# First chunk's MLP sums over 4, 5 and 5 tiles, later casts of its weights, phases of seven units from unit 18

## The chip, the cores and the metric

The kernel runs on one core of a Trainium2 chip. The metric is the device time of one execution in microseconds (us), and lower is better. TensorE (PE in the profile, with PEld for its weight loads) multiplies, ScalarE (ACT) computes exponentials and some copies, VectorE (DVE) does the elementwise work, GpSimd (POOL) and SyncE (SP) issue transfers; SPq in a row is SP's queue of transfers.

## The reference

Two branches read the same `x` of 2048 rows by 512. Branch A is attention with 32 heads of width 16 that share one key and one value head; branch B is an MLP with 1792 hidden features (14 tiles of 128) and a squared ReLU. A sigmoid gate per row mixes them.

```python
q = (x @ wq).reshape(B, S, H, Dh); k = x @ wk; v = x @ wv
p = softmax(einsum("bhqd,bkd->bhqk", q, k) * Dh ** -0.5)
a = einsum("bhqk,bkd->bhqd", p, v).reshape(B, S, H * Dh) @ wo
h = relu(einsum("bsd,df->bsf", x, w1) + b1); b = einsum("bsf,fd->bsd", h * h, w2) + b2
g = sigmoid((x * gate_w).sum(-1)); out = g * a + (1 - g) * b
```

## The kernel before

The rows are worked in four chunks of 512 (`NC`, `CH`). The attention is cut into 1024 **units** `u`: a group of four heads, 128 keys and 256 of the 512 queries. A unit has score products on TensorE (L836), one exponential of 128 by 1024 on ScalarE (L873), and eight context products that add into one bank (L893). Half of the score products land in a single spare bank `x`, from which VectorE copies them to SBUF before ScalarE takes the exponential there (`score_copy`, L857).

All other products are **filler** (L1209), cut into **slots** of half a product each: the query projection of the four chunks (16 fillers of 12 slots, the first one before the loop), the MLP's hidden tiles (`hidden`, 12 slots: 4 row tiles by three terms, since an fp32 factor is split into a rounded part and a rest), the MLP's sums (`summed`, three slots for each hidden tile summed over, four column blocks of 128 rows), and the output projection. A **span** pairs the upper half of one filler with the lower half of the filler before, so it has as many slots as the longer of the two: 12, 15 and less at the end.

A **phase** scores `n` units while it runs slots of a span in an order from the table `PLANS`, and then runs the context products of `m` earlier units (`context`); scores run four units ahead of the contexts (`AHEAD`). `block` picks `m`. In the profile a phase ends with a run of L893 products, eight to a unit: x32, x48, x56, x64 or x72 in a row of the chain are 4, 6, 7, 8 and 9 units. Below unit 32 `block` calls `exact`, which picks sizes so that a phase ends at unit 32; after a span that carried the small norm products (L425, `late`), it takes six units; a 15-slot span takes eight, or nine once the MLP's weights are all in place (`wide`).

The order on every engine is the order in which the Python code emits instructions. A planner keeps estimated times `at_pe`, `at_act`, `at_dve` of three engines, and uses them only to decide where side work goes: `spend` puts VectorE's side jobs where its estimate fits.

**The MLP's weights** come as fp32 tiles of 256 KB, two halves (w1 and w2) of each of 14 tiles. `w_load` (L487) issues a load on SP into one of two staging places, `wf` and `stage`; `w_round` casts it into `w1p` or `w2p`, on ScalarE (L525) or VectorE (L510); `w_rest` takes the rounded part off (VectorE, L519), writes the pair to DRAM for the later chunks (L521), and marks the half as wanted, so that the next load is issued at the end of that phase. `w_ready` (L535) decides at the end of a phase whether a loaded tile may be cast: the planner's TensorE time must be more than `LANDS` = 6.0 past its value at the issue of the load. If a product needs a tile that has no cast yet, `have_round` and `have` emit the cast and the rest on VectorE at that place.

`mlp` (from L792) runs the 14 hidden tiles of a chunk in the groups of `GROUPS`; behind the first hidden tile of a group it runs the four sums of the group before. `gate` (L546) computes the sigmoid, two small exponentials on ScalarE and four small VectorE instructions for each of `g` and `omg` taken together; it stands in the list `soon`, from which `spend` and the start of a span (`begin`) take.

SP also carries the query tiles: each query filler's result is written to DRAM in two parts of 256 KB, `qs<-qr` by SP (L369) and `qs<-ql` by GpSimd; `q_load` (L446) reads a head group back in eight transfers.

Of the kernel before, what the change touches and what calls it, by code (L numbers as in the profile page):

```python
# [34 lines left out]
LW = 4 * CH // 64  # L35
LANDS, DIVIDES, WRITES, SPREADS, SURE = 6.0, 10.0, 14.0, 24.0, 1.4
PAIR, CONTEXT, TURN, EXP, COPY, LATE = 0.235, 0.429, 0.36, 0.925, 0.66, 0.3
GROUPS = (0, 1, 2, 3, 4), (5, 6, 7, 8, 9), (10, 11, 12, 13)
AHEAD = 4
WHOLE, FIRST, SECOND, LATER = range(4)  # L40
EXACT = {15: ((8, 15), (7, 15)), 12: ((7, 12), (6, 12), (4, 6)), 9: ((6, 9), (4, 5))}
# [128 lines left out]
def mix_kernel(ctx: ExitStack, tc: tile.TileContext, xT, wkv, wq, wo, w12, b1, b2, cst, out):  # L170
# [67 lines left out]
    with fast, tc.tile_pool(name="at", bufs=1) as at, \  # L238
# [211 lines left out]
        wf, since, rounded, ws = ({}, {}), ({}, {}), ({}, {}), ({}, {})  # L450
# [9 lines left out]
        at_pe, at_act, at_dve = 0.0, 0.0, 0.0  # L460
# [74 lines left out]
        def w_ready(half):  # L535
            n = len(rounded[half])
            return (n == len(ws[half]) and n in since[half] and n < min(room[half], NF)
                    and at_pe - since[half][n] > LANDS)

        def wq_round(t):  # L540
            nc.scalar.activation(wqr[:, t], wqf[t], AF.Copy)
# [166 lines left out]
        def hidden(c, f, hs):  # L708

            n = c * NF + f  # L710
            while c not in x:
                chores.pop(0)[1]()
            (wr, wl), (r, l) = have_round(0, n), x[c]

            def rest(p):
                have(0, n)
                return wl[:, p]

            begun[0] += 1

            def done(p):
                hr, hl = hs[f] = ring[n % 6]
                nc.vector.tensor_scalar(h[0], p, b1t[:, f:f + 1], 0.0, op0=OP.add, op1=OP.max)  # L723
                nc.vector.tensor_tensor(h[0], h[0], h[0], OP.mult)  # L724
                split(hr, hl, h[0])
                dve(1.9)
                room[0] += 1
                if f == NF - 1 and c < 2:
                    x_again(c + 2)

            ks = [(k, slice(k * 128, (k + 1) * 128)) for k in range(KT)]
            return ([(wr[:, p], x) for k, p in ks for x in (r[:, k], l[:, k])]
                    + [(lambda p=p: rest(p), r[:, k]) for k, p in ks], done, None)
# [47 lines left out]
        def mlp():  # L781

            before, rest = None, []
            for c in range(NC):
                for fs in GROUPS:
                    hs = {}
                    for f in fs:
                        yield hidden(c, f, hs)
                        if f == 3:
                            res[c] = keep.tile(sh, F32, name=f"res{c}", tag="r0")  # L790
                            biases.extend((c, j) for j in range(4))
                        o_ready(c)  # L792
                        if c == NC - 1:
                            ask(c, 2)
                        if f == fs[0] and before:
                            if fs == GROUPS[1] and c > 1:
                                yield from projection(c - 2)
                            yield from summed(*before)
                        elif c > 0 and f > fs[0] and osp.get(c - 1) and c - 1 not in over:
                            p = projection(c - 1)  # L800
                            if c == NC - 1:
                                rest.append(p)
                                for _ in range(3):
                                    yield next(p)
                            else:
                                yield from p
                    before = c, fs, hs
            yield from rest[0] if rest else projection(NC - 2)
            yield from summed(*before)
# [222 lines left out]
        def o_ready(c):  # L1032

            if c == 0 and not wos:
                wos.extend(xp.tile(sh, F32R, name=n, tag=t) for n, t in (("wor", "xr2"), ("wol", "xl2")))

                def load(a):
                    nc.sync.dma_start(stage(), wo[a * 256:a * 256 + 256].rearrange("(t p) n -> p t n", p=128))
                    return WRITES

                for t in range(KT):
                    if t % 2 == 0:
                        chores.append((0.0, lambda t=t: load(t // 2)))
                    later(lambda t=t: wos[0][:, t], lambda t=t: wos[1][:, t], lambda t=t: stage()[:, t % 2])
            if c > 0:
                ask(c - 1)

        def ask(c, n=KT):
            if c in asked or any((c, t) not in complete for t in range(n)) or c > len(asked):
                return  # L1050
            if c and not used[c - 1]:
                return
            asked.add(c)
            tiles = []

            def load(a):
                if a == 0:
                    tiles.extend((keep.tile(sh, F32R, name="orr", tag="r3"), xp.tile(sh, F32R, name="orl", tag="xl3")))
                m = min(2, n - 2 * a)
                i = c * NG + 4 * a  # L1060
                nc.sync.dma_start(stage()[:, :m], oTs[i:i + 2 * m].rearrange("(t u) d n -> (u d) t n", u=2))
                return DIVIDES

            for t in range(n):
                if t % 2 == 0:
                    chores.append((0.0, lambda t=t: load(t // 2)))
                later(lambda t=t: tiles[0][:, t], lambda t=t: tiles[1][:, t], lambda t=t: stage()[:, t % 2],
                      (lambda: osp.update({c: tuple(tiles)})) if t == n - 1 else None)
# [23 lines left out]
        def projection(c):  # L1092
            if c in over:
                return
            over.add(c)
            yield from wait(c)
            units = list(outproj(c, ots, *osp[c], *wos))
            yield from units[:3]
            terms, done, ahead = units[3]

            def last(p):
                done(p)
                used[c] = True

            yield terms, last, ahead
# [130 lines left out]
        def phase(slots, n, m):  # L1236
# [48 lines left out]
            for half in halves():  # L1285
                if spans > 5 and w_ready(half):
                    if at_act + 0.64 < at_pe + 0.7 + CONTEXT * m:
                        w_round(half, scalar_copy)
                    elif at_dve + 0.6 < at_pe + 0.7 + CONTEXT * m:
                        w_round(half, nc.vector.tensor_copy)  # L1290

        def exact(rest, slots, later):

            def price(rest, size, later):

                if rest == 0:
                    return 0.0, None
                options = []
                for m, n in EXACT[size]:
                    parts = [n] if n == size or rest == 4 else [n, size - n]  # L1300
                    if m * len(parts) <= rest and not (later and m == 7):
                        t = sum(TURN + CONTEXT * m + PAIR * m for k in parts)
                        options.append((t + price(rest - m * len(parts), 12, False)[0], (m, n)))
                return min(options, default=(1e9, (min(rest, 6), size)))

            return price(rest, slots, later)[1]

        def block(u):
            rest, left = total - u, span.left()
            if span.slots < 7 or left < 7:  # L1310
                m = 4 if left > 3 or left == 3 and u < total - NK else 2
                if rest - m == 2:
                    m = rest
                return min(m, rest), left
            if span.slots == 15:
                long[0] -= 1
            if rest <= 16 or u < 32:
                return exact(min(rest, 32 - u) if u < 32 else rest, left, late or u < 18)
            if left <= 9:
                return 6, left  # L1320
            if span.slots == 15:
                return 9 if wide and u > wide[0] else 8, left
            halved[0] += (total - 8 - u - 9 * long[0] + max(long[0] - 30, 0)) / max(units_left[0] - long[0] + 1, 1) - 7
            halved[0] = min(max(halved[0], -1.5), 1.5)
            if late:
                return 6, left
            if halved[0] <= -1.0:
                halved[0] += 1.0
                return 6, left
            if halved[0] >= 1.0 and len(ws[1]) >= NF:  # L1330
                halved[0] -= 1.0
                return 8, left
            return 7, left

        long = [10 * NC]
        late, halved, units_left = [], [0.0], [NC * (NF + 12) + 15 + 16]
# [10 lines left out]
        u, begun_q = 0, set()  # L1347
# [67 lines left out]
```

## Time and profile before

| | us |
|---|---|
| median of three runs | 1207.36 |
| lowest, highest | 1207.36, 1207.86 |
| the profiled execution | 1208.71 |
| its span, first to last instruction | 1206.9 |
| ACT, DVE busy | 1024.7, 672.0 |
| POOL busy | 56.9 |

The profile is that of one execution, so its times add up to its own 1208.71, of which 1.8 lie outside the span. Times in its rows count from the first instruction. A row of a timeline is start, duration, engine, line, operation and operands, and in brackets the idle time of the engine just before it with what ended it. A row of the chain of waits is start, duration and what the last-ending work waited for at that moment. The granted clock (PEclk) is the share of TensorE's full clock.

### The profile page before, as it was taken

The numbers are of one execution on the slowest core, as the hardware profiler recorded it, in microseconds if no ns is written. First come the engines' busy times: TensorE is split into PE (matmuls) and PEld (weight loads), VectorE is DVE, ScalarE is ACT, GpSimd is POOL, SyncE is SP. The second block draws the span as 40 slices with busy tenths as digits, with TensorE's granted clock in tenths as the row PEclk, the third lists the DMA queues.
The fourth block names the chain that finished last, engine by engine and source line by source line (L and its number), as shares of the span: only waits on it lengthen the run. The fifth ranks groups of instructions, "written<-read, shape, count | busy, mean of one in ns | idle before, by whom it ended". The sixth has DMA issues, their size and how long they took to land.

```text
span 1206.9 us, 31970 instructions
## 1 busy us (share of the span) xinstructions
PE 1183.6 (98%) x13814; PEld 782.7 (65%) x13815; DVE 672.0 (56%) x1110; ACT 1024.7 (85%) x1134; POOL 56.9 (5%) x101
## 2 busy tenths in 40 slices
PE   9997999999999999999999999999999999999996
PEld 4665666666666666666666666666666666666663
DVE  6774678476464744463556734553647448345543
ACT  6786899898888888888888898888888888988873
POOL 1000100000000000100000000000000000010000
PEclk9998999999999999999999999999999999999999
DMA  7656344134263422330344414221515135031101
GB/s 239 204 156 196 99 146 154 52 123 156 66 219 103 155 72 85 102 98 29 121 154 151 128 40 151 90 63 37 160 56 164 46 97 168 21 107 58 58 38 38
DMA packets 55226, 132.71 MB, mean 110 GB/s; under 512 B 14554, under 2 KB 15050, under 8 KB 54568
## 3 DMA queue, kind: packets, MB, share of 16 engines
q1 hardware_dynamic: 44232, 107.58, 28.4%
q0 software_dynamic: 10704, 22.77, 5.9%
q8 instruction: 110, 1.80, 0.7%
q14 instruction: 36, 0.29, 0.1%
q10 hardware_dynamic: 144, 0.26, 0.1%
HBM read 85.88 MB, written 40.09 MB: 104 GB/s over the span
## 4 chain that ended last, share of the span: by engine, by line
PE 94%; DMA 3%; DVE 1%; ACT 1%; issue 1%; SPq 0%; DVEq 0%; ACTq 0%
PE acc L893 37%; PE mm L1209 32%; PE s L836 18%; PE x L836 5%; DMA wf<-in_w 1%; ACT e L873 1%; DMA qs<-qr 1%; DMA xf<-in_xT 0%; PE mm L310 0%; PE mm L210 0%; DVE e L857 0%; DMA w1kept<-w1p 0%; PE s L320 0%; PE s L1028 0%; PE x L976 0%
## 5 line engine op out<-in xcount | busy, mean ns | idle before, releaser
L873 ACT ACTIVATE e<-s 128x1024 f32<-128x1024 f32 x764 | 742.9, 1023 | 99.8 <-PE s L836 97.7
L857 DVE COPY e<-x 128x512 f32<-128x512 f32 x520 | 359.3, 691 | 471.3 <-PE x L836 342.6
L893 PE MATMUL acc<-e,v_ext 128*32 128x256 f32 x8192 | 470.8, 381 | 0.0
L836 PE MATMUL s<-qa,k_aug 49*128 49x512 f32 x1528 | 427.8, 413 | 7.1 <-ACT e L873 6.9
L893 PEld LDWEIGHTS acc<-e,v_ext 128*32 128x32 f32 x8192 | 252.0, 110 | 191.3 <-issue 39.3
L873 ACT ACTIVATE e<-e 128x1024 f32<-128x1024 f32 x260 | 274.1, 1058 | 27.2 <-DVE e L857 27.0
L836 PEld LDWEIGHTS s<-qa,k_aug 49*128 49x128 f32 x1528 | 220.8, 185 | 107.8 <-ACT e L873 73.4
L1209 PE MATMUL mm<-w2p,hr 64*128 64x512 f32 x1128 | 241.7, 393 | 1.8 <-DVE w2p L510 1.2
L836 PE MATMUL x<-qa,k_aug 49*128 49x512 f32 x520 | 215.7, 415 | 3.7 <-DVE o L985 1.8
L1209 PEld LDWEIGHTS mm<-w2p,hr 64*128 64x128 f32 x1128 | 156.5, 186 | 20.0 <-DVE w2p L510 1.5
L1209 PE MATMUL mm<-xragain,w1p 64*128 64x512 f32 x448 | 120.8, 393 | 0.0
L836 PEld LDWEIGHTS x<-qa,k_aug 49*128 49x128 f32 x520 | 95.6, 184 | 37.5 <-DVE e L857 13.9
L1209 PE MATMUL mm<-xr,w1p 64*128 64x512 f32 x448 | 116.0, 393 | 0.2 <-DVE w1p L519 0.2
L1209 PEld LDWEIGHTS mm<-xragain,w1p 64*128 64x128 f32 x448 | 69.6, 186 | 5.7
L1209 PEld LDWEIGHTS mm<-xr,w1p 64*128 64x128 f32 x448 | 68.6, 186 | 5.9 <-DVE w1p L519 0.7
L1209 PE MATMUL mm<-xlagain,w1p 64*128 64x512 f32 x224 | 67.8, 392 | 0.0
L1209 PE MATMUL mm<-xl,w1p 64*128 64x512 f32 x224 | 65.7, 392 | 0.0
L1209 PE MATMUL mm<-more 64*128 64x512 f32 x216 | 58.8, 392 | 0.0
L723 DVE TENSOR_SCALAR big<-mm,b1t 128x512 f32<-128x512 f32 x56 | 41.5, 742 | 0.8 <-PE mm L1209 0.8
L724 DVE TENSOR_TENSOR big<-big 128x512 f32<-128x512 f32 x56 | 38.7, 692 | 1.9
L1209 PE MATMUL mm<-wor,orr 64*128 64x512 f32 x120 | 39.1, 400 | 0.5 <-DVE ol L1018 0.5
L1209 PE MATMUL mm<-wor,orl 64*128 64x512 f32 x120 | 38.7, 393 | 0.0
(163 smaller groups left out, 795.0 us busy)
## 6 DMA issues: line engine op xcount, KB each, us to landing
w1p<-w1kept SPq DMA_DIRECT2D x42, 512.0 KB
w2p<-w2kept SPq DMA_DIRECT2D x35, 512.0 KB
qa<-qs SPq DMA_DIRECT2D x186, 64.0 KB
w1kept<-w1p SPq DMA_DIRECT2D x14, 512.0 KB
w2kept<-w2p SPq DMA_DIRECT2D x12, 512.0 KB
qs<-qr SPq DMA_DIRECT2D x16, 256.0 KB
ress<-res POOLq DMA_DIRECT2D x4, 1024.0 KB, 4.8
qs<-ql POOLq DMA_DIRECT2D x15, 256.0 KB, 8.0
```

Of the source, the lines that this page charges most:

```text
L723: nc.vector.tensor_scalar(h[0], p, b1t[:, f:f + 1], 0.0, op0=OP.add, op1=OP.max)
L724: nc.vector.tensor_tensor(h[0], h[0], h[0], OP.mult)
L836: nc.tensor.matmul(dst.rearrange("p (a n) -> p a n", a=2), k_aug[rows, kt * 128:(kt + 1) * 128], qa[it][rows, :, q * HC:q * HC + HC], star ...
L857: nc.vector.tensor_copy(e_half(u)[:, 2 * r:2 * r + 2], x.rearrange("p (a n) -> p a n", a=2))
L873: nc.scalar.activation(e_half(u), src, AF.Exp, scale=SCALE)
L893: nc.tensor.matmul(accs[q][h * 32:(h + 1) * 32], v_ext[:, kt], es[u][:, h % 2 * 2 + h // 2], start=kt == 0 and it > 0, stop=kt == NK - 1, ...
L1209: nc.tensor.matmul((self.before if r else self).bank, a[p], b[p], start=not r and i == 0, stop=r == 1 and i == len(self.terms[1]) - 1, ski ...
```

## The change

Three edits. `GROUPS` becomes a list with an entry per chunk, and the first chunk's groups are of 4, 5 and 5 hidden tiles, not 5, 5 and 4. `w_ready` asks for twice `LANDS`. `block` no longer calls `exact` below unit 32: below unit 18 the rule is six units, and from there on the rule of all later units.

```diff
-GROUPS = (0, 1, 2, 3, 4), (5, 6, 7, 8, 9), (10, 11, 12, 13)
+GROUPS = [[(0, 1, 2, 3), (4, 5, 6, 7, 8), (9, 10, 11, 12, 13)]] + [[(0, 1, 2, 3, 4), (5, 6, 7, 8, 9), (10, 11, 12, 13)]] * 3
...
-                    and at_pe - since[half][n] > LANDS)
+                    and at_pe - since[half][n] > 2 * LANDS)
...
-                for fs in GROUPS:
+                for fs in GROUPS[c]:
...
-                            if fs == GROUPS[1] and c > 1:
+                            if fs[0] == 5 and c > 1:
...
-            if rest <= 16 or u < 32:
-                return exact(min(rest, 32 - u) if u < 32 else rest, left, late or u < 18)
+            if rest <= 16:
+                return exact(rest, left, late)
+            if u < 18:
+                return 6, left
```

**ScalarE, spans 7 to 9 (before) and 7 to 10 (change), the casts of the third and fourth w2 tile.** Before, from the cast of the second w1 tile on:

```order
L525 ACTIVATE w1p<-stage 128x512
L873 ACTIVATE e<-s 128x1024 x3
L873 ACTIVATE e<-e 128x1024
L873 ACTIVATE e<-s 128x1024
L873 ACTIVATE e<-e 128x1024
L873 ACTIVATE e<-s 128x1024
L525 ACTIVATE w2p<-wf 128x512
L873 ACTIVATE e<-s 128x1024 x5
L873 ACTIVATE e<-e 128x1024
L525 ACTIVATE w2p<-stage 128x512
```

The change, from the same cast on:

```order
L525 ACTIVATE w1p<-stage 128x512
L946 ACTIVATE accs<-acc 128x256
L873 ACTIVATE e<-s 128x1024 x3
L873 ACTIVATE e<-e 128x1024
L873 ACTIVATE e<-s 128x1024
L873 ACTIVATE e<-e 128x1024
L873 ACTIVATE e<-s 128x1024 x6
L873 ACTIVATE e<-e 128x1024
L525 ACTIVATE w2p<-wf 128x512
```

Seven exponentials stand between the two casts before, and 13 in the change; the cast of the fourth w2 tile follows seven exponentials after that, against six before.

**VectorE, the first sums over the second group of the first chunk (span 31 before, 30 in the change).** Before, behind the evaluation of a hidden tile (L203):

```order
L203 TENSOR_TENSOR hr<-big,hr 128x512
L510 CAST w2p<-wf 128x512
L857 COPY e<-x 128x512
L519 TENSOR_TENSOR w1p<-stage,w1p 128x512
L857 COPY e<-x 128x512
L519 TENSOR_TENSOR w2p<-wf,w2p 128x512
L921 TENSOR_SCALAR n<-lq 128x32
L857 COPY e<-x 128x512
L510 CAST w2p<-stage 128x512
L922 SCALAR_TENSOR_TENSOR lq,ok<-n,lq 128x32
L857 COPY e<-x 128x512
L519 TENSOR_TENSOR w2p<-stage,w2p 128x512
```

The change, at its first sums over the second group:

```order
L203 TENSOR_TENSOR hr<-big,hr 128x512
L510 CAST w2p<-wf 128x512
L857 COPY e<-x 128x512
L519 TENSOR_TENSOR w1p<-wf,w1p 128x512
L857 COPY e<-x 128x512
L519 TENSOR_TENSOR w2p<-wf,w2p 128x512
L857 COPY e<-x 128x512 x2
L723 TENSOR_SCALAR big<-mm,b1t 128x512
```

The cast of a second w2 tile and its rest, which stood before among the copies of the same phase, are gone from it: there the tile is cast on ScalarE at the end of the phase.

**VectorE, the gate (span 5 before, span 15 in the change).** Before:

```order
L857 COPY e<-x 128x512 x2
L549 TENSOR_SCALAR g<-g 128x16
L550 RECIPROCAL g<-g 128x16
L549 TENSOR_SCALAR omg<-omg 128x16
L550 RECIPROCAL omg<-omg 128x16
L857 COPY e<-x 128x512 x2
```

The change:

```order
L410 TENSOR_TENSOR sq_147<-qr 128x512
L549 TENSOR_SCALAR g<-g 128x16
L550 RECIPROCAL g<-g 128x16
L549 TENSOR_SCALAR omg<-omg 128x16
L550 RECIPROCAL omg<-omg 128x16
L857 COPY e<-x 128x512 x4
```

The four instructions move from the start of the second phase of span 5, ahead of its two copies, to the start of span 15, ahead of its four copies.

## The prediction

> **What bounds the kernel now.** I read the page first, for the engine that sets the end.
>
> ```profile
> PE 1183.6 (98%) x13814; PEld 782.7 (65%) x13815; DVE 672.0 (56%) x1110; ACT 1024.7 (85%) x1134; POOL 56.9 (5%) x101
> PE 94%; DMA 3%; DVE 1%; ACT 1%; issue 1%; SPq 0%; DVEq 0%; ACTq 0%
> ```
>
> TensorE is busy for 98% of the span and makes 94% of the chain of waits. The change takes no product away, so it can save only two things: the time in which TensorE stands still or runs slowly, and time lost between products where phases are cut badly. The waits of TensorE say where it stands.
>
> ```profile
> PE s L836 <- ACT e L873: 6.9, 2, 6.5
> PE mm L1209 <- DVE w2p L510: 1.2, 1, 1.2
> PE mm L1209 <- DVE w2p L519: 0.7, 1, 0.7
> ```
>
> One wait of 6.5 us stands out, for an exponential. The next question is what held ScalarE there, so I took its timeline, and SP's.
>
> ```profile
> 88.13 0.63 ACT L525 ACTIVATE w2p<-wf 128x512 fp32r<-128x512 f32 x1 [2.17 <-DMA wf<-in_w]
> 102.00 0.63 ACT L525 ACTIVATE w2p<-stage 128x512 fp32r<-128x512 f32 x1 [7.60 <-DMA w1kept<-w1p]
> 90.11 2.42 SPq L487 DMA_DIRECT2D stage<-in_w  x2
> 77.35 10.10 DMA wf<-in_w
> 89.36 8.81 DMA qs<-qr
> ```
>
> ScalarE stands at two weight casts, 2.17 and 7.60 us. The row of the second names the write `w1kept`, issued last before it, but the cast reads `stage`, whose loads SP issued from 90.11 on. The wait for those fits: by the chain (the last two rows), the first pair took 10.10 us from its issue at 77.35, and 90.11 to 102.00 are 11.9. A planner's distance of 6 is too short for loads that queue among the query writes, which need 8.81 us themselves. Behind the cast on ScalarE stand the exponentials of the next phase, and behind those TensorE's score banks.
>
> TensorE's own timeline shows the price, by the starts of phases. The rows of 126.51 and later are from the chain.
>
> ```profile
> 86.19 0.40 PE L425 MATMUL x<-sq,blk 128*32 128x512 bf16 x4
> 94.99 0.50 PE L836 MATMUL s<-qa,k_aug 49*128 49x512 f32 x1
> 103.86 0.80 PE L836 MATMUL s<-qa,k_aug 49*128 49x512 f32 x2 [6.50 <-ACT e L873]
> 110.97 0.43 PE s L836
> 118.73 0.43 PE s L836
> 126.51 0.22 PE x L425 x4
> 133.84 0.66 PE s L836 x2
> ```
>
> From 86.19 to 94.99 a six-unit phase behind norm products takes 8.80; the same kind takes 7.33 from 126.51 to 133.84: **1.47 lost**. From 94.99 to 110.97 a seven-unit phase takes 15.98; the next, to 118.73, takes 7.76: **8.22 lost**, 1.72 more than the idle 6.50. The stretches tell why.
>
> ```profile
> 100.00:101.00 1.00, 0.00 (x0) 0.00 (x0) 0.00 (x0) 0.00 (x0) 0.00 (x0) 0.52 0.95 381
> 105.00:106.00 1.00, 1.00 (x8) 0.81 (x6) 0.00 (x0) 1.00 (x2) 0.00 (x0) 0.50 0.43 107
> 107.00:108.00 1.00, 1.00 (x16) 0.51 (x16) 0.15 (x1) 0.56 (x1) 0.00 (x0) 1.00 0.88 246
> ```
>
> The granted clock (third figure from the end) falls to half while TensorE waits, and is back only at 107, three us after its products start. A long wait is thus dearer than it looks; a short one need not be. The Trainium skill, TensorE: Matmul & The Clock Gate, Part 1, says that about 3.4 us of idleness halve the clock and about 3.4 us of work restore it. The trace agrees (idle from 97.4, half clock from 100, full again 3.1 us after 103.86). By that rule a wait under 3 us costs its length alone.
>
> **The change part by part.** *Later casts.* By the order, the third w2 tile's cast on ScalarE falls a phase later behind its load, and so does the fourth's: a phase is 7.8 us, so 2.17 is covered outright. The 1.47 goes. For the fourth it is close. Before, SP issued its load 3.9 us after the phase start at 86.19, and it was there at 102.00, 15.8 after that start. ScalarE came to the cast at 94.40 (102.00 less 7.60), 8.2 after it, of which up to 1.5 are the stall that goes, so 6.7; a phase more makes 14.5. In the change the end of the first head group falls one phase later, so two small transfers slip in ahead of this load, `oc` and `lq`:
>
> ```profile
> 71.54 0.54 SPq L953 DMA_DIRECT2D oc<-accs  x1
> 72.13 0.61 SPq L954 DMA_DIRECT2D lq<-accs  x1
> ```
>
> With 1.15 for them the load is there at about 17, and ScalarE waits about 2.4 (17.0 less 14.5), much as it did for the third tile. That 2.17 cost TensorE 1.47; I take **1.4** for it. The bounds are 0 (it lands sooner, with fewer weight writes among the transfers) and the whole 8.22. So the edit gives 1.47 + 8.22 − 1.4.
>
> *No casts forced by a product.* Before, two places emit VectorE work because a product needs it at once. The chain shows them:
>
> ```profile
> 262.06 3.16 PE acc L893 x56
> 267.69 0.69 DVE w1p L519
> 270.33 3.16 PE acc L893 x56
> 277.50 0.35 DVE w2p L510
> 281.44 3.59 PE acc L893 x64
> 201.44 3.59 PE acc L893 x64
> 210.65 3.59 PE acc L893 x64
> ```
>
> From one run of seven units' context products to the next are 8.27 us (262.06 to 270.33) where 7.76 is the rule (110.97 to 118.73, above): **0.51**. From the end of that run (273.49) to the end of the next (281.44 + 3.59 = 285.03) are 11.54, where eight units with 15 slots take 9.21 (201.44 to 210.65): **2.33**. In the changed order the forced cast and rest of the second w2 tile are gone from VectorE's row of copies, and every L519 has its cast in an earlier phase. Since the first sums take four tiles and not five, the second sums begin a phase earlier, and start with tile 4, so tile 9 is not needed there at all. Together the stalls that go are 1.47 + 8.22 + 0.51 + 2.33 = **12.5**.
>
> *Phases.* Counting the runs of context products in the two orders, the change has two of four units fewer, as many of six, three more of seven, five fewer of eight and three more of nine: 138 for 139, with the same units, slots and copies. Of the five of eight, two ran 12 slots and three 15; one of six runs behind norm products in place of a plain one. Prices, from ends of such runs (start plus duration):
>
> ```profile
> 50.92 2.73 PE acc L893 x48
> 57.07 1.86 PE acc L893 x32
> 61.77 1.86 PE acc L893 x32
> 68.05 2.73 PE acc L893 x48
> 342.03 3.16 PE acc L893 x56
> 350.25 3.60 PE acc L893 x64
> 434.08 4.03 PE acc L893 x72
> 444.00 4.02 PE acc L893 x72
> ```
>
> The two of four took 58.93 − 53.65 = 5.28 and 63.63 − 58.93 = 4.70, a plain six 70.78 − 63.63 = 7.15, a late six 7.33, a seven 7.76, an eight in 12 slots 353.85 − 345.19 = 8.66, in 15 slots 9.21, a nine 9.92. The sum: −5.28 − 4.70 − 7.15 + 7.33 + 3 × 7.76 − 2 × 8.66 − 3 × 9.21 + 3 × 9.92 = **−1.7**. It comes mostly from the two of four, ten us for work that one eight does in 8.7. Bounds: 0, if the new sevens keep ScalarE or VectorE busier than the later ones do, and −2.1, the halved span's 1.3 (5.28 + 4.70 − 8.66) and twice the other terms' 0.4.
>
> *The gate* moves to span 15's start, ahead of four copies.
>
> ```profile
> 59.42 0.17 DVE L549 TENSOR_SCALAR g<-g 128x16 f32<-128x16 f32 x1 [1.85 <-ACT g L548]
> 59.95 0.25 DVE L550 RECIPROCAL omg<-omg 128x16 f32<-128x16 f32 x1
> 134.41 0.69 DVE L857 COPY e<-x 128x512 f32<-128x512 f32 x1 [1.32 <-PE s L836]
> ```
>
> The four take 0.8 us (59.42 to 60.20), behind up to 1.85 of waiting for ScalarE's part. VectorE is idle 1.32 before a phase's first copy, which hides the instructions, and only a wait behind ScalarE's queue shows. I take **0.4**, from 0 (hidden whole) to 1.3 (0.8 and 1.85 less 1.32).
>
> The sizes of sums cost nothing by themselves: the slots are the same, the 12-slot sums only come first, and their weights (four w2 tiles) lie there long before. If w2 tile 4 or 5 were not, the cover would be gone and VectorE would cast it under the product, 2.33 as above.
>
> Sum: −12.5 + 1.4 − 1.7 + 0.4 = **−12.4**. The profiled execution, 1208.71 with 1.8 around its span, would take 1196.3; it lies 1.35 above the median, so I set the change against the median 1207.36: **1195.0**.
>
> **The rivals.** *The saved time is given back to the query writes.* Each phase up to span 16 issues 512 KB of them; a row says 8.81 for the SP half, more than a phase of 7.8. The stalls gave these writes 9.7 us to catch up. Without them loads could land later and later, and the fourth tile's wait keep its 8.22: −12.4 + 6.8 = −5.6, **1201.8**. For it: the 11.9 above. Against: writes overlap, and the mean DMA share (the figure before the last) is 0.43 to 0.95 in the three stretches above, not full throughout. A page points the other way: the Trainium skill, DMA: Bandwidth & Descriptors, in "Anatomy of one DMA — SWDGE (gpsimd) path", gives 2.0 us and bytes at 436 GB/s. As an estimate that is 2.6 us for a 256 KB load, which the old distance would cover. The trace has 10.10 and decides. Chance 0.12.
>
> *The forced casts come back elsewhere*, with the first rival: a further 2.8, so −2.8, **1204.6**. Against: no product in the new order stands ahead of its cast. Chance 0.05.
>
> *Slower: the later casts starve the hidden tiles.* A staging place is now held for three phases, not two, and there are two places per half, so w1 tiles come at one in 1.5 phases, while hidden tiles 5 to 9 use one per phase. If a load is late there, a product waits for the load, the cast and the rest, long enough to halve the clock, 8.2 each as above. Two such waits cost 16.4: −12.4 + 16.4 = +4.0, **1211.4**; it decides from the second wait on. Against: room for w1 tiles opens only as hidden tiles finish, four phases of sums lie in between, and casts stand ahead of use. Chance 0.05.
>
> **How the numbers follow.** Forecast 0.78, at 1195.0 with its own range 1192 to 1199; rivals 0.12, 0.05, 0.05. About 0.2%, 2.4 us, is what a measurement can tell from no change, so faster means below 1204.9 and slower above 1209.8. The first two cases are faster, and half of the third: 0.92; the same 0.03; slower 0.05. The lower end takes the fourth tile's wait and the gate at 0 and the phases at −2.1 (1207.36 − 14.6 = 1192.8), with one us of small waits that may also go: 1191.8. The upper end reaches to the first rival, 1202.
>
> **What would show it.** Right: no ScalarE wait over 3 us at L525 and no wait of TensorE over 2 us between 60 and 110; PEclk in the fourth of the 40 slices at 9; no TensorE wait for `w2p` near 265; a span near 1194.5. The fourth tile's cast with a wait of 1 to 3 us would confirm that term. Wrong: a stretch of half clock after 60 us, TensorE waiting for L510 or L519, or six- and seven-unit phases above 7.4 and 7.9 where they are new.

## The result, and the profile after

| | before | after |
|---|---|---|
| median of 20 runs each, us | 1209.99 | 1210.16 |
| lowest, highest | 1203.86, 1216.32 | 1204.93, 1223.5 |
| ratio to before, 95% interval | | 1.0006 [0.9988, 1.0024] |
| the profiled execution, its span | 1208.71, 1206.9 | 1208.67, 1206.9 |

The time did not change; 1195.0 was forecast. Twenty runs of the kernel before also spread over 1%, where the three shown ahead of the prediction lay within 0.04%. Here and below a ratio leaves out runs over 1.5% above the fastest of their kernel, as the 1223.5 is, and a median takes in all. The two profiled spans are equal, so the time saved in one place must have been lost in another. The page of the kernel after shows one hollow, as the page before did:

```profile
PE 1182.7 (98%) x13815; PEld 782.5 (65%) x13815; DVE 672.7 (56%) x1110; ACT 1025.2 (85%) x1134; POOL 56.7 (5%) x101
PEclk9999899999999999999999999999999999999998
PE 92%; DMA 4%; DVE 1%; ACT 1%; issue 1%; SPq 0%; ACTq 0%; DVEq 0%
```

The granted clock dips in the fifth of 40 slices, 120.7 to 150.9 us. Four rows from the waits of three engines of the kernel after, from 60 to 180 us (total, times, longest), say what is new:

```profile
PE x L836 <- DVE e L857: 9.9, 2, 9.5
ACT w2p L525 <- DMA stage<-in_w: 1.9, 1, 1.9
DVE n L921 <- DMA lq<-accs: 10.3, 1, 10.3
DVE g L549 <- ACT g L548: 1.1, 1, 1.1
```

The 7.60 at a weight cast is down to 1.9, and no row of TensorE for `w2p` is left. In their place VectorE stands 10.3 us at L921, which starts the division of the sums. When a pair of head groups has its sums, ScalarE copies them to `accs` (L946), SP transfers the values to `oc` and the denominators to `lq` (L953, L954), VectorE takes the limits and the reciprocal of `lq` (L921, L922, L916), GpSimd spreads the result through DRAM into `lc`, and VectorE multiplies `oc` by `lc` (L925). The timelines of the kernel after, on VectorE, ScalarE and SP:

```profile
117.36 0.68 DVE L519 TENSOR_TENSOR w2p<-wf,w2p 128x512 fp32r<-128x512 f32 x1
128.35 0.18 DVE L921 TENSOR_SCALAR n<-lq 128x32 f32<-128x32 f32 x1 [10.30 <-DMA lq<-accs]
...
128.68 0.69 DVE L857 COPY e<-x 128x512 f32<-128x512 f32 x1
...
131.59 1.02 ACT L873 ACTIVATE e<-s 128x1024 f32<-128x1024 f32 x1 [10.79 <-PE s L836]
...
108.66 2.06 SPq L369 DMA_DIRECT2D qs<-qr  x1
110.78 0.99 SPq L487 DMA_DIRECT2D stage<-in_w  x1
111.87 12.76 SPq L446 DMA_DIRECT2D qa<-qs  x8
124.72 0.52 SPq L953 DMA_DIRECT2D oc<-accs  x1
125.29 0.58 SPq L954 DMA_DIRECT2D lq<-accs  x1
```

VectorE runs in order. Behind L921 stand the copies of the scores (L857), behind them TensorE's spare bank, and behind that ScalarE's exponentials: one small transfer holds three engines. SP needed 12.76 us to issue eight reads ahead of it. The transfer itself is the smaller part; its row in the chain of waits of the kernel after:

```profile
125.29 3.03 DMA lq<-accs
```

The same places in the kernel before:

```profile
128.38 0.18 DVE L921 TENSOR_SCALAR n<-lq 128x32 f32<-128x32 f32 x1 [0.44 <-DMA lq<-accs]
...
118.35 7.09 SPq L446 DMA_DIRECT2D qa<-qs  x8
125.56 0.67 SPq L953 DMA_DIRECT2D oc<-accs  x1
126.27 0.58 SPq L954 DMA_DIRECT2D lq<-accs  x1
```

Both kernels run L921 at 128.4. Before, the stalls at the two casts had held VectorE back until `lq` was nearly there, so only 0.44 of waiting showed. Without them VectorE comes ten us sooner and waits ten us.

What TensorE lost is read from the runs of context products in its timeline and, in the third group, in the chain of waits (kernel after):

```profile
96.15 3.23 PE L893 MATMUL acc<-e,v_ext 128*32 128x256 f32 x56
105.00 3.23 PE L893 MATMUL acc<-e,v_ext 128*32 128x256 f32 x56
112.78 3.23 PE L893 MATMUL acc<-e,v_ext 128*32 128x256 f32 x56
...
257.23 3.23 PE L893 MATMUL acc<-e,v_ext 128*32 128x256 f32 x56
265.97 3.66 PE L893 MATMUL acc<-e,v_ext 128*32 128x256 f32 x64
275.20 3.66 PE L893 MATMUL acc<-e,v_ext 128*32 128x256 f32 x64
```

```profile
131.49 4.02 PE acc L893 x48
```

From the end at 116.01 (112.78 + 3.23) to the end at 135.51 are 19.50 for six units behind norm products, which take 7.33: **12.2 lost**. The windows of the kernel after show how 9.5 of waiting became 12.2 (the stretch and its length, PE busy, PEld, DVE, ACT, POOL, granted clock, DMA share, GB/s):

```profile
116.00:120.00 4.00, 3.90 (x35) 2.80 (x29) 1.72 (x3) 3.23 (x5) 0.00 (x0) 1.00 0.35 109
120.00:124.00 4.00, 0.00 (x0) 0.00 (x0) 0.00 (x0) 0.80 (x1) 0.69 (x1) 0.98 0.18 61
124.00:128.00 4.00, 0.00 (x0) 0.00 (x0) 0.00 (x0) 0.00 (x0) 0.00 (x0) 0.50 0.48 90
128.00:132.00 4.00, 2.58 (x15) 1.51 (x19) 2.80 (x8) 0.41 (x1) 1.28 (x2) 0.50 0.41 114
132.00:136.00 4.00, 4.00 (x52) 1.98 (x46) 1.12 (x2) 1.56 (x2) 0.00 (x0) 0.74 0.79 208
```

The clock falls to 0.50 and stays there after the products resume; 48 context products take 4.02, not 2.73. The second thing to see is the DMA share beside the wait: 0.18 to 0.48. VectorE waits for a transfer while the DMA engines are on average more than half idle.

### The profile page after: what moved, and what is told of

Same layout as the page of the kernel before. It is cut to its first block, busy times and chain, and to the rows that moved or that the text cites. A ratio compares the mean times of both kernels' runs of the same rounds, so it can differ in the third digit from the quotient of the medians.

```text
span 1206.9 us, 31976 instructions
## 1 busy us (share of the span) xinstructions
PE 1182.7 (98%) x13815; PEld 782.5 (65%) x13815; DVE 672.7 (56%) x1110; ACT 1025.2 (85%) x1134; POOL 56.7 (5%) x101
## 4 chain that ended last, share of the span: by engine, by line
PE 92%; DMA 4%; DVE 1%; ACT 1%; issue 1%; SPq 0%; ACTq 0%; DVEq 0%
PE acc L893 37%; PE mm L1209 31%; PE s L836 18%; PE x L836 5%; DMA stage<-in_w 2%; ACT e L873 1%; DMA qs<-qr 1%; DVE e L857 0%; DMA qa<-qs 0%; DMA xf<-in_xT 0%; PE mm L310 0%; PE mm L210 0%; DMA wf<-in_w 0%; DMA lq<-accs 0%; PE s L320 0%
## 5 line engine op out<-in xcount | busy, mean ns | idle before, releaser
L857 DVE COPY e<-x 128x512 f32<-128x512 f32 x520 | 359.6, 692 | 470.7 <-PE x L836 354.5
```

What stands on the lines that cost most here:

```text
L857: nc.vector.tensor_copy(e_half(u)[:, 2 * r:2 * r + 2], x.rearrange("p (a n) -> p a n", a=2))
```

## The experiments

Two theories were set against each other. **The margin theory** (theory C in the expectations): in the first 175 us transfers land late by an amount that differs from execution to execution; a late transfer costs nothing until some engine, working in order, comes to its reader, and the reader with the least margin pays for all. **Its rivals** put the lateness down to one place: SP's order, the shape of a write, the room for GpSimd's descriptors, the number of transfers that SP may have in flight; or they hold that the new order of phases itself makes the stall. All medians below are of the runs beside the kernel before on the same chip; "lost" is the time of a phase above its kind's normal one.

### The division later, and the same kernel profiled three times

```diff
# e1_divide_later, e1_second_look, e1_third_look: the kernel after with
-    divisions.extend(divide(o, l, 4 * c + t, at_act + (LANDS if (c, t) == (NC - 1, 2) else DIVIDES)))
+    divisions.extend(divide(o, l, 4 * c + t, at_act + (LANDS if (c, t) == (NC - 1, 2) else 2 * DIVIDES)))
```

> The changed kernel, with VectorE's division of a head group (L921 and what follows) placed 20 and not 10 planner units after its sums are copied. TensorE's and ScalarE's orders are the same as in the changed kernel; VectorE's alone differs. Theory A (the whole saving was lost at one place: L921, first in VectorE's order of span 13, waits 10.3 us for a transfer that SP issues behind eight reads): no wait of VectorE over 1 us at L921, the phase of 19.50 us back near 7.3, and the time 11 to 12 us below the changed kernel, a ratio to the kernel before near 0.990. Rival B (the first fillers' stretch is bound by the transfers, so a stall only moves to the next reader of them): another wait of 6 us or more on a transfer between 100 and 170 us, and the time within 3 us of the kernel before, a ratio of 0.998 to 1.002.

> The kernel of e1_divide_later again, for a second profile: its times spread from 1195.5 to 1217.1, and the one execution profiled took 1197.5. Theory C (the transfers of the first fillers' stretch land several us earlier or later from one execution to the next, so that waits with a margin of a few us turn into stalls in some executions): if this execution takes over 1203, its profile shows one or more waits of 3 us or more on a transfer between 60 and 175 us (the casts of the third to fifth w2 tile, or L921), with half clock behind them, and the rest of the phases as in the first profile. Rival D (the spread is elsewhere, in TensorE's clock or in products that take longer): no such wait, and longer phases or a lower granted clock after 175 us.

> A third profile of the kernel of e1_divide_later, with the same expectations as the second: by theory C a time over 1203 goes with waits of 3 us or more on transfers between 60 and 175 us; by rival D it goes with longer phases or a lower clock after 175 us.

Twelve runs: 1205.76, ratio 0.9966 [0.9936, 0.9995], with the runs in that ratio from 1195.5 (mean granted clock 0.999) to 1213.16 (0.988). The ratio lies between the ranges named for theory A and for rival B and meets neither. The three profiled spans of this one kernel are 1195.7, 1205.3 and 1197.5. Their longest waits for a transfer, in this order:

```profile
ACT w2p L525 <- DMA stage<-in_w: 2.7, 1, 2.7
```

```profile
DVE oc L925 <- DMA lc<-ls: 8.6, 1, 8.6
```

```profile
ACT w2p L525 <- DMA stage<-in_w: 3.7, 1, 3.7
```

L921 waits in none of them, though the phases are those of the kernel after, so its stall was the place's and not the phases'. But one program, three executions, and a different reader pays: the cast, the product with `lc`, the cast again. The execution with the longest wait is also the longest, as theory C said, but it waits at L925, which was not among the readers that the expectation named. The profile of a single execution names the reader that lost in that execution.

### SP's order, the writes' shape, GpSimd's room

```diff
# e2_read_behind: the kernel after, the reads issued behind the sums' transfers
+            context(range(u, u + m))
             it = (u + m - 1) // (2 * NK)
             if it not in begun_q and it + 1 < NC * NG:
                 begun_q.add(it)
                 q_load(it + 1)
-            context(range(u, u + m))
# e7_write_in_four: the kernel after, SP's query write (L369) as four of 32 rows
+                if eng is nc.sync and second is nc.gpsimd:
+                    for i in range(4):
+                        eng.dma_start(bass.AP(tensor=o.tensor, offset=o.offset + i * KS * 2 * CH,
+                                              ap=[[CH, 2 * DH], [1, CH]]), src[32 * i:32 * i + 32].bitcast(F32))
+                    continue
# e10_ring: the kernel after, e12_ring_before: the kernel before, both with
-            wide = at.tile([128, CH], F32, name="lc", bufs=2)
+            wide = at.tile([128, CH], F32, name="lc", bufs=1)
...
-    nc = bacc.Bacc("TRN2", target_bir_lowering=False, num_devices=1, dynamic_dma_scratch_size=1024)
+    nc = bacc.Bacc("TRN2", target_bir_lowering=False, num_devices=1, dynamic_dma_scratch_size=3072)
```

> The changed kernel, with the eight reads of the next head group (L446) issued behind the transfers of the sums (L953, L954) and not ahead of them. No other engine's order changes. Theory A1 (lq lands late because SP issues it late, behind reads that took SP 12.8 us): L921 waits under 3 us, the time 8 to 12 us below the changed kernel, a ratio near 0.991. Rival A2 (it lands late because the rings that it uses are backed up with query writes, whatever its place in SP's order; the reads issued at 111.9 landed at 124 too): lq issued near 112 lands at 122 to 125, L921 still waits 5 to 7 us, and the gain is 3 to 5 us, a ratio near 0.996.

> The changed kernel, with SP's half of each query tile's write (L369) issued as four transfers of 32 rows, not one of 4 by 32 rows. The same bytes; the orders of the computing engines stay. Theory R (the one write keeps a few rings busy for 7 to 15 us and everything behind it on those rings waits): the weight loads land 3 to 5 us after their issue and not 8 to 14, the wait of 1.9 us at the fourth w2 cast and most of the 10.3 us at L921 go, ratio 0.988 to 0.992. Rival Q (SP and its limit of transfers in flight are the bottleneck, not rings): three more issues per query tile delay SP by some 2 us each, L921 waits longer, ratio 1.000 to 1.004.

> The changed kernel, with three times the space for the descriptors of GpSimd's transfers (3072 for 1024 bytes a partition, made room for by one buffer of lc in place of two). Every engine's order is that of the changed kernel. Theory G (GpSimd issues a query write only when the one before has landed, 7 to 11 us each against phases of 7.8, because its descriptors have no more room; that chain falls behind once the stalls are gone): its writes are issued as VectorE finishes them, two or more in flight, and L921 in span 13 or L925 wait less; ratio 0.992 to 0.998. Rival H (the DMA engines themselves are full, the order of issue does not matter): the writes overlap but each takes longer, SP's transfers land as late or later, L921 still waits 8 to 12 us; ratio 0.999 to 1.005.

> The kernel before, with the larger descriptor space alone; every order as before. It has the casts one phase behind their load, so by theory C its stalls at the third and fourth w2 cast stay (they wait for SP's loads): ratio 0.998 to 1.003. By theory G, if GpSimd's writes in turn are what makes the loads late, the 8.2 us stall at the fourth cast shrinks: ratio 0.992 to 0.997. By rival H the loads land later and the stalls grow: ratio 1.002 to 1.008.

| kernel | median, before's | ratio, 95% interval | longest waits for a transfer (line numbers of the kernel after) |
|---|---|---|---|
| e2_read_behind | 1207.76, 1209.82 | 0.9986 [0.9966, 1.0005] | L921 7.0, cast 2.6 |
| e7_write_in_four | 1211.06, 1209.82 | 1.0022 [1.0008, 1.0037] | L921 8.5, `accs` L946 3.9 |
| e10_ring | 1207.75, 1209.19 | 0.9993 [0.9962, 1.0023] | L921 7.0, `accs` 3.5, cast 2.6 |
| e12_ring_before | 1210.94, 1209.19 | 1.0007 [0.9982, 1.0031] | casts 4.1 and (put down to "issue") 3.9, L921 2.6 |

None of the three, changed alone, takes the stall away. The timelines of SP and VectorE in e2 show it most plainly for SP's order:

```profile
118.52 0.59 SPq L954 DMA_DIRECT2D lq<-accs  x1
...
127.77 0.18 DVE L921 TENSOR_SCALAR n<-lq 128x32 f32<-128x32 f32 x1 [6.99 <-DMA lq<-accs]
```

`lq` is issued 6.8 us sooner than in the kernel after (118.52 for 125.29), and read 0.6 us sooner (127.77 for 128.35). In these two executions the transfer that was issued earlier was there at about the same time: 9.25 us from its issue to its reader in e2 (118.52 to 127.77), where it took 3.03 in the kernel after. So its place on SP alone does not say when it lands. With more room the wait of GpSimd's query writes ends with VectorE's `ql`, where the profile had put it down to "issue" (no cause that it shows); the timelines of GpSimd, first in the kernel after and then in e10:

```profile
111.93 0.70 POOL L369 DMA_DIRECT2D qs<-ql  x1 [10.76 <-issue]
```

```profile
112.41 0.69 POOL L369 DMA_DIRECT2D qs<-ql  x1 [8.75 <-DVE ql L407]
```

Nothing came of it, nor of SP's write in four parts, where L921 still waited 8.5. By their ratios e7 fits rival Q and e10 rival H, but L921 waits less than in the kernel after in both (8.5 and 7.0 for 10.3), and neither rival named that; rival Q, a limit of SP's transfers in flight, is not excluded. e2's wait of 7.0 is what rival A2 named, without the gain that it named; e12's ratio fits theory C.

### One edit of the change alone

```diff
# e3_lands_only: the kernel before with
-                    and at_pe - since[half][n] > LANDS)
+                    and at_pe - since[half][n] > 2 * LANDS)
```

> The kernel before, with the doubled distance of the casts alone. Theory A: the stalls of 1.5 and 8.2 us at the third and fourth w2 cast go, but then the transfers come later relative to the products, and L921 in span 13 waits 6 to 10 us: the time within 4 us of the kernel before, a ratio of 0.997 to 1.001. If instead the new wait at L921 comes from the other two edits (a head group's end that falls a phase earlier or later), this kernel gains nearly all of the 9.7 us: a ratio near 0.992.

Twelve runs: 1211.1, ratio 1.002 [0.9999, 1.0041]. In its profile a w2 cast waits 4.0 (4.66 lost), L921 3.2 (6.08 lost), and the casts forced by a product are there as before (2.32 lost). Of the 9.7 lost at two casts before, part is still lost at a cast, and a new loss stands at L921, without the change's phases and sums: these are not needed for it. The ratio lies just above the range of theory A, and far from the 0.992 of its rival.

### Margin for one reader after another

```diff
# e6_both: e1 and e2 together
# e8_three_behind: e1 and
-                    and at_pe - since[half][n] > 2 * LANDS)
+                    and at_pe - since[half][n] > (3 if spans < 17 else 2) * LANDS)
# e9_multiply_later: e8 and (L925 of the first sums)
-                    (0.72, ready + (SPREADS if i < LAST_OK - 1 else LANDS + 4.0), lambda: nc.vector.tensor_tensor(o, o, wide, OP.mult)))
+                    (0.72, ready + (2 * SPREADS if i == 0 else SPREADS if i < LAST_OK - 1 else LANDS + 4.0), lambda: nc.vector.tensor_tensor(o, o, wide, OP.mult)))
# e11_ring_later: e9 and the room of e10
# e13_all_margins: e11, the reads behind as in e2, and (use of the output weights)
-                    return WRITES
+                    return 2 * WRITES
# e15_weights_later: e11 and
-                    return WRITES
+                    return 1.5 * WRITES
```

> The kernel of e1_divide_later, with the reads of the next head group issued behind the transfers of the sums as in e2_read_behind. By theory C the casts' waits are what is left, and these transfers are not among them: a median within 3 us of e1's 1205.8, ratio 0.994 to 0.999. If VectorE's division or ScalarE's reuse of the sums' buffer still waits for oc or lq in some executions, it is 3 to 6 us better than e1.

> The kernel of e1_divide_later, with the casts of the weights three planner distances (18) behind the issue of their load as long as query tiles are written (up to span 16), and two after. Theory C: the casts' margins grow by a phase of 7.8 us, few executions stall at them, and the times close up near the best of e1: a median of 1195 to 1199, most runs below 1200, ratio 0.987 to 0.992. If the spread of e1 comes from another wait or from the clock, the median stays near 1205, ratio 0.995 to 0.998.

> The kernel of e8_three_behind, with the multiplication of the first division (L925, which waited 5.3 us in e8, 8.6 in e1's second look and 11.1 in e6 for lc, a transfer in GpSimd's queue) placed 48 and not 24 planner units behind its place before. Theory C (each reader of a transfer in this stretch stalls when its margin is a few us, and the stalls do not move on once every such reader has a margin of a phase or more): no wait of VectorE or ScalarE on a transfer over 2 us between 60 and 330, most runs between 1194 and 1199, ratio 0.985 to 0.991. Rival B (the stretch is bound by the transfers): a new reader waits 5 us or more, the median stays near 1205, ratio 0.994 to 0.998.

> The kernel of e9_multiply_later with the larger descriptor space of e10_ring. By theory C alone it is as e9, within 2 us, since all waits have margins. By theory G it also closes up the slow runs that e9 still has: median 1194 to 1198. By rival H, if SP's loads land later through more GpSimd traffic, waits at the casts come back and it is 2 to 6 us slower than e9.

> The kernel of e11_ring_later, with the eight reads of the next head group issued behind the two transfers of the sums, and the output weights' use a phase and more later behind their load. Theory (the saving is given to whichever in-order reader has the least margin behind a transfer): with the last two readers given margin no wait for a transfer above 3 us is left before 330 us of the profile, and the median is 1194 to 1198, ratio 0.986 to 0.990. Rival (each margin only moves the stall to a new reader): a wait of 4 us or more for some other transfer, and a median of 1199 or more, ratio 0.991 or above.

> The kernel of e11_ring_later with the output weights' use half a distance further behind their load (21 and not 14). Theory (every reader with margin, no forced cast): the 5.1 that e11 lost at the output weights is gone, no wait of TensorE over 1 us before 330 us but for the gate's, span 1193 to 1196, median 1195 to 1198, some 2.5 us under e13, ratio 0.986 to 0.989. Rival (another reader is late in its place): a wait for a transfer of 3 us or more, median 1198 or above, ratio 0.990 or above.

| kernel | median, before's | ratio, 95% interval | profiled span | longest wait for a transfer on ACT or DVE after 60 us |
|---|---|---|---|---|
| e6_both | 1205.88, 1209.2 | 0.9968 [0.9937, 0.9999] | 1204.8 | L925 for `lc` 11.1 |
| e8_three_behind | 1204.9, 1209.2 | 0.9951 [0.992, 0.9981] | 1199.2 | L925 for `lc` 5.3 |
| e9_multiply_later | 1200.25, 1209.19 | 0.992 [0.9892, 0.9948] | 1199.6 | `accs` L946 5.3 |
| e11_ring_later | 1198.71, 1209.19 | 0.9909 [0.9879, 0.9939] | 1199.8 | output weights L643 4.1 |
| e13_all_margins | 1198.28, 1211.28 | 0.9899 [0.9869, 0.9929] | 1196.6 | none |
| e15_weights_later | 1196.9, 1209.88 | 0.9894 [0.9871, 0.9917] | 1194.0 | `accs` L946 2.2 |

Each margin takes its reader off the list and another one pays; from e6 to the end of the table the longest wait falls from 11.1 to 2.2, with none in e13. The intervals of neighbours in the table overlap, those of e6 and e13 do not. e8's gain is a miss for theory C, which put its median at 1195 to 1199: in its profile no cast waits any more, but L925 does. The waits of e9 and of e11:

```profile
ACT accs L946 <- DMA lq<-accs: 5.3, 1, 5.3
```

```profile
DVE wor L643 <- DMA stage<-in_wo: 4.1, 1, 4.1
```

In e13 no such wait is left on VectorE or ScalarE after the first 60 us, and its ratio lies in the range expected for it, though its median is 0.3 above. The waits of TensorE show what is left:

```profile
PE mm L1209 <- DVE w2p L510: 1.1, 1, 1.1
PE mm L1209 <- DVE w2p L519: 0.7, 1, 0.7
```

The later output weights had moved VectorE's side jobs, and a cast forced by a product was back (2.3 lost). In e15, where it stands ahead of its product again, the granted clock by the page shows no hollow; below it TensorE's waits after 60 us, and the timelines of SP and VectorE:

```profile
PEclk9999999999999999999999999999999999999999
```

```profile
PE s L836 <- ACT e L873: 1.4, 1, 1.4
```

```profile
110.41 16.05 SPq L446 DMA_DIRECT2D qa<-qs  x8
126.55 0.52 SPq L953 DMA_DIRECT2D oc<-accs  x1
127.12 0.67 SPq L954 DMA_DIRECT2D lq<-accs  x1
...
132.78 0.17 DVE L921 TENSOR_SCALAR n<-lq 128x32 f32<-128x32 f32 x1
```

This is the strongest row for the margin theory. In the kernel with the lowest median the eight reads take 16.05 us to issue (12.76 in the kernel after) and `lq` goes out at 127.12, later than in the kernel after. The transfers are issued as late as ever; L921 runs at 132.78 and waits for nothing. TensorE keeps one wait of 1.4, where none above 1 was expected. Span and median lie in their ranges, and the ratio just above its own. The median lies 1.4 under e13's, not 2.5, and no more than the kernel before differs between their two chips: beside the kernel before, each is 13.0 lower (1211.28 − 1198.28 and 1209.88 − 1196.9). What the cast forced in e13 cost is thus not seen in the medians.

### The margins without the rest of the change

```diff
# e14_margins_alone: the kernel before with the margins of e13, except that the casts take
-                    and at_pe - since[half][n] > LANDS)
+                    and at_pe - since[half][n] > (3 if spans < 17 else 1) * LANDS)
```

> The kernel before with all the margins of e13 (later casts in the first sums, later division, first product with the sums, reads behind the sums' transfers, later output weights, larger descriptor room), without the change's sums of 4, 5 and 5 tiles and its phases of seven. Theory: the margins alone bring back the stalls of the two casts, 9.7, less what the new waits keep; the two casts that a product forces remain (2.8) and the phases' 1.7 is not gained, so it stands some 4.5 us behind e13: ratio 0.990 to 0.994. Rival (the phases and the sums bring nothing by themselves): it equals e13 within 0.2%. Rival (the phases are what makes the room): a ratio of 0.997 or above.

Measured: 1199.76 beside 1211.28, ratio 0.9907 [0.9874, 0.994], span 1198.2. With the margins alone the time of the casts' stalls is saved, as the theory said. It stands only 1.5 behind e13 and not 4.5, which also meets the condition of the first rival (equal to e13 within 0.2%); e13 has a forced cast too, and e15's span, of one execution, is 4.2 shorter. The intervals of the three ratios overlap, so the times do not tell the theory from that rival, and what the sums and phases bring on top rests on the profiles.

## Why the prediction was wrong, point by point

- **Stalls that go, 12.5: right, each.** The third cast's 1.47 is gone: the six units behind norm products there take 7.33 in the kernel after (from 84.27 to 91.60, ends of runs of context products), and the seven units after them 7.78 (to 99.38). Of the fourth cast's 8.22 only the next point is left. No forced cast is left: from 260.46 to 269.63 and on to 278.86 the phases of eight units take 9.17 and 9.23, where 9.21 is the rule.
- **The new wait at the fourth cast, 1.4:** from 99.38 to 108.23 are 8.85 for seven units, about 1.1 lost, with ScalarE waiting 1.9 (2.4 was named; 17.0 less 14.5 is 2.5).
- **Phases, −1.7:** the size fits as far as a balance can tell. The two spans are equal, and −12.5 with the losses read here, 1.1, 12.2 and 0.6, makes +1.4, so about −1.4 is left for the phases and whatever was not read by itself.
- **The gate, 0.4:** 0.6 lost, with VectorE waiting 1.1 for ScalarE's part. The whole of it lies in the bounds given.
- **The step that failed: what comes late next.** The sum took the removed stalls as saved, after looking at the next wait of one reader only, the fourth cast. It saw `oc` and `lq` move ahead of a load, and priced them as 1.15 for that load; it did not ask who reads `lq`. The row to look at was in the profile before: L921 had waited 0.44, so it had no margin, and any time that VectorE gained ahead of it had to be waited out there. This wait, 10.3 on VectorE and 9.5 on TensorE, had no term in the sum. The loss, 12.2, cancels the 12.5 nearly whole.
- **The first rival was the right mechanism at the wrong place.** It said that the stalls had given the transfers time and that this would be given back. It was tied to the cast, priced at 6.8, and given 0.12. What spoke against it, a DMA share of 0.43 to 0.95 that is not full, was no argument: while L921 waited, the share was 0.18 to 0.48. The other two rivals did not come: no row of TensorE's waits names a cast or a load of the MLP's weights.
- **The signs named.** Of those for a right forecast all came but the span: no wait over 3 us at L525, none of TensorE over 2 us between 60 and 110, the fourth slice of the granted clock at 9, no wait for `w2p` near 265. They watched the places that the change touched. The one that caught the error was the general one, a stretch of half clock after 60 us.
- **The sum fits a kernel whose readers have margin, in its total.** e15 has the change's three edits, one of them stretched further, and margins besides; its span of 1194.0 is near what the prediction named for a right forecast (1194.5), and its median is 13.0 under that of before on its chip, for −12.4. That does not prove the terms one by one: the margins without the sums and phases already give 11.5 (e14, 1211.28 − 1199.76).

Why the transfers of the first 175 us land late and unevenly is open. Excluded as the whole cause are SP's order, the shape of SP's query writes and GpSimd's descriptor room; not tried were a kernel without the query writes and one with fewer transfers in flight on SP.

## What to carry to other kernels

A stall ahead of an in-order engine is cover for every transfer that the engine reads later. Before counting its removal as a gain, list the next readers of transfers on that engine, and the wait of each in the profile: one that waits little but above zero has no margin and will take the stall over. A wait of zero is no proof of margin either: L925 waits for nothing in the profiles before and after, and 8.6 and 11.1 us in e1_second_look and e6_both. When several executions of one kernel differ by a per cent, profile it more than once: here three profiles of one program named two different readers, and giving all those readers margin (e13, e15) saved more than the one repair of L921 (e1).

## What the hardware showed

A wait under 3 us is not always cheap. In e1_third_look TensorE waits once for ScalarE, 2.59 us, and loses 4.4. Its timeline and its windows:

```profile
104.08 0.62 PE L836 MATMUL s<-qa,k_aug 49*128 49x512 f32 x2 [2.59 <-ACT e L873]
```

```profile
102.00:103.00 1.00, 0.00 (x0) 0.00 (x0) 0.00 (x0) 0.51 (x1) 0.00 (x0) 1.00 0.73 111
...
104.00:105.00 1.00, 0.92 (x6) 0.73 (x8) 0.00 (x0) 1.00 (x3) 0.00 (x0) 0.66 0.90 269
105.00:106.00 1.00, 1.00 (x8) 0.82 (x6) 0.00 (x0) 1.00 (x2) 0.00 (x0) 0.50 0.78 225
106.00:107.00 1.00, 1.00 (x6) 0.79 (x6) 0.69 (x1) 0.80 (x1) 0.00 (x0) 0.50 0.81 295
107.00:108.00 1.00, 1.00 (x8) 0.65 (x4) 0.00 (x0) 0.21 (x1) 0.00 (x0) 0.64 0.60 205
```

The clock is still full while TensorE waits, and falls to half only after its products have begun again, for some three us. In e1_divide_later, the same kernel, the wait was shorter, left the clock at 1.00 and lost 1.8:

```profile
PE s L836 <- ACT e L873: 1.6, 1, 1.6
```

Other profiles narrow it: a wait of 2.19 us in e12_ring_before, which ends at 105.72, is followed by a granted clock of 0.50 from 106 to 109, and one of 2.43 in e10_ring, which ends at 96.55, by 0.50 from 97 to 99. The Trainium skill, TensorE: Matmul & The Clock Gate, Part 1, puts the fall behind at least one idle window of about 3.4 us, and says that the window runs freely; the prediction took from it that a wait under 3 us costs its length alone. The late fall would fit a window that closes after the wait, but 2.59 us of idleness do not fill one, nor do 2.19, and there the measurement decides. The prediction's own row did not agree either: idle from 97.4 and at half clock from 100 are 2.6 us. Its inference did not decide this forecast, since the wait that it had no term for lasted 9.5.
